# Attention scores computed three head pairs ahead of the top-k search instead of two, with six score buffers instead of five

## The chip, the cores and the metric

The kernel runs on one core of one Trainium2 chip. The metric is the device time of one execution in microseconds (us). Three executions of the kernel before took 788.19, 790.3 and 794.51 us, a median of 790.3 us. A smaller number is better.

## The reference

Three layers follow each other, on 1152 tokens (2 batches of 576) with 512 features (8 heads of 64):

```python
scores = scale * q @ k.T                        # per batch and head, 576 x 576
kth    = np.partition(scores, -32)[..., -32]    # the 32nd largest of each row
attn   = softmax(where(scores >= kth, scores, -1e9))
x      = attn @ v                               # back to 1152 x 512
h      = x @ w_in                               # 512 x 2048
x      = (h * tanh(softplus(h))) @ w_out        # 2048 x 512
x      = ((x @ w_a) * (x @ w_b)) @ w_out2       # 512 x 1536, twice, then back
```

The inputs are 8 bytes wide for the weights and 4 bytes wide for q, k and v.

## The kernel before

**Attention.** The 1152 rows of q are cut into nine tiles of 128 rows (tile 4 holds the last 64 rows of both batches), and the eight heads into four pairs. One (tile, pair) is a step; there are 36. A step has three parts:

- `scores` (lines 159 to 179). `prep_q` transposes q on TensorE (`pq`, L144), splits it into a high part on ScalarE (`qh`, L154) and a low part on VectorE (`ql`, L155). For tiles 0 and 4, `prep_k` also loads, splits and transposes that pair of k (L107 to L128; its low part is made by GpSimd for batch 0 and by VectorE for batch 1, and `ks`, `kr`, `km`, `kn` have one buffer each). Eight matmuls (sixteen for tile 4) into `psc` follow (L176), and four ScalarE copies bring them to the tile `s2` of the step (L178).
- `largest` (lines 181 to 199), the search. On VectorE four rounds of MAX8 (L192) for the two heads and three of match-and-replace (L195) find the 32 largest of each row: 8 and 6 passes over 576 columns.
- `weighted_sum` (lines 205 to 251). The masked exponentials are made on VectorE (L212) and ScalarE (L217 to L220), transposed on TensorE (`pe`, L227), copied (`et`, L228) and multiplied with v (`px`, L234). After a tile's fourth pair the row sums are applied (`x`, L250).

**Weights.** All 68 weight blocks arrive as 8-byte numbers and are turned into 4-byte ones by ScalarE, VectorE and GpSimd (`convert`, L283 to L306), stored in device memory, and loaded again each time they are used (`raw`, L325). Where a layer works in two parts, `weight` splits a block into `whl` on ScalarE or VectorE (L332, L334) and GpSimd (L335).

**The two feed-forward layers.** `gated` and `bilinear` run three times (`PLAN`): over tiles 0, 1, 2 (the first layer as tiles 0 and 1, then tile 2), over 3, 4, 5, and over 6, 7, 8. The matmuls are L362 (into `ph`) and L369 (into `acc` and `po`). A group's gate needs `x` of its tiles, its bilinear layer the transposed results (`pt`, L351).

**What sets the order.** The program writes the three streams of work down interleaved: `together` draws a quarter of a step from `attention` and a block of weights or of a layer in turn, by the quotas of `STEPS`. `attention` (lines 253 to 268) writes the scores of the first `ABUF[7]` steps before the first search. Then each step writes its search in four rounds; after round 0 it writes the weighted sum of the step before, and after round 1 the scores of the step `ABUF[7]` later. A planner in the build then gives each engine its fixed order: what is written earlier goes first, and `PRI` moves parts forward in that order (scores by 200 places, L160; weighted sums by 300, L202; layer activations by 30; the end of a tile by 100), as far as operands and buffers allow. On the chip each engine works through its order strictly and waits for its operands. All DMAs are issued from SP. `ps` (L78) gives three PSUM banks to `pq`, `pk`, `pr`, `psc`, `pe`, `px`, `prs` and `pt` together. `ABUF[0]` is the number of `s2` buffers (L169), `ABUF[1]` that of `wk`, `ABUF[2]` that of `e2`, `ABUF[4]` that of `qh` and `ql`.

```python
ahead = [scores(*z) for z in steps[:ABUF[7]]]
...
    if r == 0 and tail:
        weighted_sum(*tail)
    if r == 1 and i + ABUF[7] < len(steps):
        ahead.append(scores(*steps[i + ABUF[7]]))
```

Of the kernel before, what the change touches and what calls it, by code (L numbers as in the profile page):

```python
# [33 lines left out]

SIGN = (4, 4)

ABUF = (5, 3, 2, 1, 2, 3, 1, 2)
COPIES = (0, 0, 0, 1, 4, 2)

CONV = (26, 28, 20, 2)  # L40
# [11 lines left out]
def topk_attention_mlps(ctx: ExitStack, tc: tile.TileContext, q, k, v, w, out):  # L52
# [22 lines left out]
    wp = ctx.enter_context(tc.tile_pool(name="wp", bufs=1))  # L75
    ep = ctx.enter_context(tc.tile_pool(name="ep", bufs=ABUF[5]))
    dp = ctx.enter_context(tc.tile_pool(name="dp", bufs=1, space=DRAM))
# [28 lines left out]
    def prep_k(b, hp):  # L106
        ks = wp.tile([P, 2, J, D], F32, name="ks", bufs=BUFS[4])  # L107
        kr = wp.tile([R, 2, D], F32, name="kr", bufs=BUFS[4])
        for s in range(2):
            nc.sync.dma_start(ks[:, s], k[b, 2 * hp + s, 0:SM, :].rearrange("(p j) d -> p j d", j=J))  # L110
        nc.sync.dma_start(kr, k[b, 2 * hp:2 * hp + 2, SM:S, :].rearrange("h p d -> p h d"))
        km = wp.tile([P, 2, J, 2, D], F32R, name="km", bufs=BUFS[4])
        kn = wp.tile([R, 2, 2, D], F32R, name="kn", bufs=BUFS[4])
        for z, raw in ((km, ks), (kn, kr)):
            high, low = (z[..., i, :] for i in range(2))
            nc.scalar.copy(high, raw)
            (nc.gpsimd, nc.vector)[KSUB[b]].tensor_sub(low, raw, high.bitcast(F32))
        for s in range(2):
            kk = kks[:, (b * H + 2 * hp + s) % (H + 2), :]
            pk = bank("pk")  # L120
            for j in range(J):
                nc.tensor.transpose(pk[:, j * P:(j + 1) * P], km[:, s, j].rearrange("p z d -> p (z d)").bitcast(F32),
                                    ident)
            pr = bank("pr", R)
            nc.tensor.transpose(pr, kn[:, s].rearrange("p z d -> p (z d)").bitcast(F32), ident[:R, :R])
            for src, o, n in ((pk, s * R, SM), (pr, SM * (1 - s), R)):
                nc.scalar.copy(kk[:, o:o + n], src)  # L127
            KK[b, 2 * hp + s] = kk  # L128
# [12 lines left out]
    def prep_q(t, hp):  # L141
# [4 lines left out]
        for b, o, n in ([(t // (J + 1), 0, P)] if t != J else [(b, b * R, R) for b in range(B)]):  # L146
            qh = att.tile([P, 2, P], F32R, name="qh", bufs=ABUF[4])
            ql = att.tile([P, 2, P], F32R, name="ql", bufs=ABUF[4])
            if n != P:
# [13 lines left out]
    def scores_(t, hp):  # L163
# [3 lines left out]
        if t in (0, J):  # L167
            prep_k(t // J, hp)
        s2 = att.tile([P, 2, S], F32, name="s2", bufs=ABUF[0])  # L169
        for s in range(2):  # L170
# [10 lines left out]
    def largest(s2):  # L181

        e2 = att.tile([P, 2, S], F32, name="e2", bufs=ABUF[2])
        wk = att.tile([P, 2, S], F32, name="wk", bufs=ABUF[1])
        m8 = att.tile([P, 2, TOPK], F32, name="m8")
# [332 lines left out]
```

## Time and profile before

| | |
|---|---|
| runs | 788.19, 790.3, 794.51 us; median 790.3 |
| profiled execution | 790.78 us, of which the span of the instructions is 789.0 |
| busy over the span | TensorE 690.1 us (87%), VectorE 571.1 (72%), ScalarE 550.8 (70%), GpSimd 466.0 (59%) |
| granted TensorE clock, mean | 0.935 |

Busy shares are means over stages that differ, so the rows below cut the span into stages. A matmul's duration is modelled and overlaps the next one's, so that the sum of durations is more than the time they take. A number in brackets after an instruction is the time its engine stood idle before it, with what ended that.

### The profile page before, as it was taken

The page shows a single profiled execution, that of the slowest core. Times are in us where ns is not written, and L with a number is a line of the kernel's source. Part 1 is how long each engine was busy: PE and PEld are TensorE (multiplying, and loading weights), DVE is VectorE, ACT ScalarE, POOL GpSimd, SP SyncE. Part 2 cuts the span into 40 slices and gives each one's busy share as a digit, 9 for nine tenths or more (in the row PEclk, how much of TensorE's full clock was granted, in tenths as well). Part 3 has the DMA queues.
Part 4 walks back from the last instruction along what each step waited for, and adds up shares of the span by engine and source line. Part 5 has one row for each costly group of instructions (what it writes and reads, how often), then busy time and mean ns, then how long its engine had stood idle before and what let it go on. Part 6 is the DMA issues. An engine that isn't in the chain of part 4 may idle for free. (4 is left out here: it accounts for less than half of the span.)

```text
span 789.0 us, 12393 instructions
## 1 busy us (share of the span) xinstructions
PE 690.1 (87%) x3988; PEld 572.0 (72%) x3988; DVE 571.1 (72%) x1152; ACT 550.8 (70%) x1262; POOL 466.0 (59%) x390
## 2 busy tenths in 40 slices
PE   3565657789977988999999999988999999989997
PEld 2444535556664757889897888867979999969996
DVE  3999999976798789986679998998601276523331
ACT  5889888888997996666668998976524275553232
POOL 6756566676775751456554465552648767665661
PEclk9987667799997998999999999997999999999999
DMA  8987665889989973134334234221403454433411
GB/s 244 288 272 251 209 204 182 225 256 304 354 282 325 342 232 111 54 95 133 94 90 129 78 90 112 80 68 55 134 15 108 119 173 125 131 105 107 125 51 40
DMA packets 79537, 126.12 MB, mean 160 GB/s; under 512 B 27504, under 2 KB 31600, under 8 KB 79472
## 3 DMA queue, kind: packets, MB, share of 16 engines
q1 hardware_dynamic: 79472, 125.33, 52.3%
q8 instruction: 31, 0.51, 0.3%
q14 instruction: 34, 0.28, 0.1%
HBM read 105.12 MB, written 20.19 MB: 159 GB/s over the span
## 5 line engine op out<-in xcount | busy, mean ns | idle before, releaser
L335 POOL TENSOR_TENSOR whl<-raw,whl 128x512 fp32r<-128x512 f32 x164 | 215.3, 1321 | 161.5 <-ACT whl L334 126.6
L192 DVE MAX8 m<-wk 128x8 f32<-128x576 f32 x216 | 158.5, 749 | 1.1
L362 PE MATMUL ph<-yh,whl 128*128 128x384 f32 x576 | 154.6, 340 | 0.7 <-ACT yh L344 0.7
L298 POOL TENSOR_TENSOR w<-w,w 128x512 int32<-128x512 int32 x68 | 89.0, 1309 | 77.8 <-DVE w L295 40.5
L362 PEld LDWEIGHTS ph<-yh,whl 128*128 128x128 f32 x576 | 105.6, 190 | 4.0 <-ACT yh L344 1.6
L195 DVE MATCH_REPLACE8 wk<-m,wk 128x576 f32<-128x576 f32 x144 | 106.4, 741 | 0.0
L362 PE MATMUL ph<-yl,whl 128*128 128x384 f32 x288 | 98.4, 342 | 0.1
L299 POOL TENSOR_TENSOR w<-w,w 128x512 f32<-128x512 f32 x68 | 89.7, 1322 | 7.0 <-ACT w L297 2.2
L234 PE MATMUL px<-et,v 128*64 128x128 f32 (+1 forms) x800 | 76.6, 297 | 17.3 <-ACT et L228 17.0
L334 ACT CAST whl<-raw 128x512 fp32r<-128x512 f32 x113 | 69.3, 622 | 28.8 <-PE ph L362 16.2
L234 PEld LDWEIGHTS px<-et,v 128*64 128x64 f32 x800 | 53.1, 151 | 40.1 <-ACT et L228 26.8
L377 POOL TENSOR_TENSOR gl<-m,gh 128x384 fp32r<-128x384 f32 x52 | 55.5, 1067 | 42.9 <-ACT gh L376 12.1
L362 PE MATMUL ph<-xh,whl 128*128 128x384 f32 x256 | 71.6, 340 | 0.7 <-DVE m L409 0.7
L192 DVE MAX8 m<-s 128x8 f32<-128x576 f32 x72 | 53.9, 751 | 25.2 <-ACT s L178 24.7
L176 PE MATMUL psc<-kks,qh 128*128 128x288 f32 x160 | 57.2, 377 | 13.8 <-ACT kks L127 7.9
L434 DVE TENSOR_TENSOR m<-ph,e 128x384 f32<-128x384 f32 x36 | 19.9, 554 | 67.9 <-PE ph L362 54.9
L376 ACT CAST gh<-m 128x384 fp32r<-128x384 f32 x68 | 34.8, 511 | 48.8 <-DVE m L434 27.6
L227 PE MATMUL pe<-ident,e 128*128 128x128 f32 x324 | 55.7, 305 | 14.7 <-ACT e L220 7.4
L176 PE MATMUL psc<-kks,ql 128*128 128x288 f32 x160 | 51.4, 352 | 11.5 <-DVE ql L155 11.2
L178 ACT COPY s<-psc 128x288 f32<-128x288 f32 x144 | 52.0, 402 | 13.2 <-PE psc L176 12.4
L293 ACT ACTIVATE w<-w 128x512 f32<-128x512 f32 x68 | 46.5, 684 | 20.3 <-DMA w<-in_w_dram 13.5
L228 ACT COPY et<-pe 128x384 f32<-128x384 f32 x108 | 50.3, 487 | 14.6 <-PE pe L227 14.5
(90 smaller groups left out, 1520.3 us busy)
## 6 DMA issues: line engine op xcount, KB each, us to landing
raw<-ws SPq DMA_DIRECT2D x229, 256.0 KB, 2.8
w<-in_w_dram SPq DMA_DIRECT2D x68, 512.0 KB, 4.8
ws<-w SPq DMA_DIRECT2D x68, 256.0 KB, 4.5
qr<-in_q_dram SPq DMA_DIRECT2D x16, 256.0 KB, 4.2
ks<-in_k_dram SPq DMA_DIRECT2D x16, 128.0 KB, 4.3
v<-in_v_dram SPq DMA_DIRECT2D x16, 128.0 KB, 3.9
out_dram<-o SPq DMA_DIRECT2D x8, 256.0 KB, 3.0
qr<-in_q_dram SPq DMA_DIRECT2D x4, 128.0 KB, 8.1
```

Of the source, the lines that this page charges most:

```text
L176: nc.tensor.matmul(psc, qq[:, s, :], kk[:, a * HS:(a + 1) * HS], start=(n == 0), stop=(n == len(parts) - 1))
L178: nc.scalar.copy(s2[:, s, a * HS:(a + 1) * HS], psc)
L192: nc.vector.max(m8[:, s, got], src[:, s, :])
L195: nc.vector.match_replace(wk[:, s, :], m8[:, s, got], src[:, s, :], NEG)
L227: nc.tensor.transpose(pe[:, i, :], ef[:, n * P:(n + 1) * P], ident)
L234: nc.tensor.matmul(px[s * D:(s + 1) * D, o:o + n], vt[b][:, 2 * hp + s, j, :] if j < J else v4[b][:, hp, s, :], et[:, i if j < J else J, o ...
L298: nc.gpsimd.tensor_tensor(wi, wi, count, op=ALU.add)
L299: nc.gpsimd.tensor_mul(wf, wf, highf)
L334: nc.scalar.copy(wh, raw)
L335: sub().tensor_sub(wl, raw, wh.bitcast(F32))
L362: nc.tensor.matmul(ph, a, x, start=(i == 0), stop=(i == len(mm) - 1))
L377: sub().tensor_sub(gl, g, gh.bitcast(F32))
```

## The change

Two numbers of `ABUF`: `s2` gets six buffers instead of five, and scores are written three steps ahead of the search instead of two. The scores of step 2 move ahead of the first search, and those of every later step move ahead by the search and the weighted sum of one step, with all that was written between.

```diff
-ABUF = (5, 3, 2, 1, 2, 3, 1, 2)
+ABUF = (6, 3, 2, 1, 2, 3, 1, 3)
```

## Rows read from the trace of the kernel before

**Rows 1.** Busy times by stage: PE, PEld, DVE, ACT, POOL, then granted clock, DMA share, GB/s
```profile
16.00:136.00 120.00, 72.85 (x392) 53.48 (x390) 117.10 (x249) 101.84 (x245) 77.42 (x62) 0.77 0.77 239
136.00:294.00 158.00, 135.90 (x692) 95.03 (x691) 129.19 (x259) 143.24 (x312) 107.43 (x90) 0.91 0.89 288
294.00:315.00 21.00, 18.32 (x158) 15.57 (x157) 19.29 (x44) 14.97 (x43) 5.00 (x11) 0.84 0.42 121
315.00:540.00 225.00, 216.42 (x1451) 187.92 (x1450) 200.19 (x415) 173.93 (x429) 121.44 (x100) 0.98 0.33 91
540.00:600.00 60.00, 59.97 (x367) 51.46 (x366) 27.23 (x55) 28.94 (x66) 30.89 (x26) 0.97 0.25 75
600.00:789.00 189.00, 180.39 (x919) 164.15 (x917) 74.25 (x129) 78.19 (x153) 115.33 (x90) 0.99 0.38 109
```

**Rows 2.** VectorE's waits (total, times, longest): 0 to 165, 165 to 320, 320 to 570
```profile
DVE m L192 <- ACT s L178: 2.5, 3, 1.7
...
DVE m L192 <- ACT s L178: 7.0, 6, 1.6
...
DVE m L192 <- ACT s L178: 15.2, 9, 4.9
```

**Rows 3.** Timeline of ScalarE and VectorE, a search's start and the last two steps
```profile
362.58 0.76 DVE L192 MAX8 m<-s 128x8 f32<-128x576 f32 x1 [4.86 <-ACT s L178]
...
548.22 0.78 ACT L218 ACTIVATE e<-s,nk 128x576 f32<-128x576 f32 x1
...
553.87 1.01 ACT L178 COPY s<-psc 128x288 f32<-128x288 f32 x3 [0.96 <-PE psc L176]
...
558.80 0.40 ACT L178 COPY s<-psc 128x288 f32<-128x288 f32 x1
...
559.24 0.76 DVE L192 MAX8 m<-s 128x8 f32<-128x576 f32 x1
```

**Rows 4.** The page's group of MAX8: busy, mean ns of one, idle before
```profile
L192 DVE MAX8 m<-wk 128x8 f32<-128x576 f32 x216 | 158.5, 749 | 1.1
```

**Rows 5.** Attention's matmuls from 315 to 540 us, by line
```profile
L234 PE MATMUL px<-et,v 128*64 128x128 f32 (+1 forms) x360 | 27.1, 263 | 1.4 <-ACT et L228 1.4
...
L227 PE MATMUL pe<-ident,e 128*128 128x128 f32 x133 | 19.9, 272 | 0.2 <-ACT s L178 0.2
...
L176 PE MATMUL psc<-kks,qh 128*128 128x288 f32 x60 | 18.1, 318 | 0.5 <-ACT qh L154 0.5
L176 PE MATMUL psc<-kks,ql 128*128 128x288 f32 x60 | 16.6, 316 | 3.9 <-DVE ql L155 3.8
...
L144 PE MATMUL pq<-ident,qr 128*128 128x128 f32 x30 | 6.6, 300 | 0.0
```

**Rows 6.** A piece of the chain that ended last: start, length
```profile
719.13 3.32 PE ph L362 x19
```

**Rows 7.** Timeline, tile 8's result and the first matmul that reads it
```profile
591.59 0.69 DVE L250 TENSOR_TENSOR x<-xr,prs 128x512 f32<-128x512 f32 x1 [8.57 <-ACT xr L238]
...
630.69 0.34 PE L362 MATMUL ph<-xh,whl 128*128 128x384 f32 x1
```

**Rows 8.** Timeline, tile 1's result and the start of the first gate
```profile
134.43 0.68 DVE L250 TENSOR_TENSOR x<-xr,prs 128x512 f32<-128x512 f32 x1
...
135.49 0.53 PE L176 MATMUL psc<-kks,ql 128*128 128x288 f32 x2 [2.35 <-DVE ql L155]
...
136.33 0.92 PE L362 MATMUL ph<-xf,w 128*128 128x256 f32 x3
```

**Rows 9.** The stretch from 520 to 540 us, columns as in Rows 1
```profile
520.00:540.00 20.00, 15.33 (x96) 11.69 (x95) 19.72 (x39) 15.51 (x39) 8.15 (x7) 0.83 0.19 54
```

**Rows 10.** Timeline of VectorE and TensorE in that stretch
```profile
533.38 0.41 DVE L155 SCALAR_TENSOR_TENSOR ql<-pq,qh 128x256 fp32r<-128x256 f32 x1
...
533.85 0.85 PE L176 MATMUL psc<-kks,ql 128*128 128x288 f32 x2 [2.77 <-DVE ql L155]
```

## The prediction

> **What bounds the kernel now.** I read the busy times by stage first, because the shares over the whole span hide that the bound changes [rows 1]. From 16 to 136 us VectorE is busy for 117.1 of 120 us: the searches of tiles 0 and 1, with the weight conversions among them, set the pace. From 136 to 294 no engine is full (ScalarE 143.2 and TensorE 135.9 of 158), but the DMA share is 0.89: the weights' conversion and reloading bind. From 294 to 315 nearly everything is attention, at a granted clock of 0.84. From 315 on TensorE is the bound, with 216.4 of 225 us, 60.0 of 60 and 180.4 of 189.
>
> Is a busy TensorE a full one? A piece of the final chain has 19 matmuls of 384 columns in 3.32 us [rows 6], 0.175 us each with no gap. So it is full there, and after 315 us only a gap that closes, or TensorE work that leaves this stage, can save time.
>
> Then I looked for what the change acts on: how long the search waits for scores, and how far ahead scores really are. VectorE waits 2.5 us for them up to 165, 7.0 from there to 320 and 15.2 from 320 to 570 [rows 2], 24.7 in all. And the scores are not two steps ahead when they run: the last step's copies begin at 553.87, after the step before it last read its own scores at 548.22, and the search starts its second head at 559.24, with the copy at 558.80 [rows 3]. The lead of the written order is used up by the planned order. So the lead is short in fact, and the buffers are not: at the end two of the five would do.
>
> **The change, part by part.**
>
> *The sixth buffer* costs and brings nothing by itself: a scores tile is free before the next but one is filled [rows 3]. The Trainium skill's page Perfetto Trace Analysis, section Optimization Strategy, says that gaps which repeat on an engine can mean that there is no room for the next tile. By that rule the buffer would be worth the waits, up to 24.7 us; the trace disagrees with it here, since the tile was free 5.65 us before it was filled (553.87 − 548.22).
>
> *Three steps written before the first search.* Step 2's k loads, splits, transposes, two matmul groups and four copies now stand ahead of the first search in the order. Moved on SP are its two `ks` loads and `kr`, past the early weight loads; on GpSimd its two subtractions, past conversions. `ks` has one buffer, so they come behind step 1's, and the first search needs step 0 alone: 0 us. Bounds: 2.5 us gained, if all waits up to 165 go [rows 2], or the same amount lost, if ScalarE serves step 2 where step 0's search waits.
>
> *The first stage* is VectorE's, and its work is unchanged but for one `ql` more, 0.41 us [rows 10], that is now done before tile 1 ends. This end matters: `x` of tile 1 comes at 134.43 and the first gate matmul at 136.33, with a score step in front of it for which TensorE waited 2.35 us [rows 8]. With the change that place is held by the next step's scores. I take 0; bounds from −2.4 us (the wait is gone) to +2.8 (0.41 + 2.35: one more of the kind).
>
> *From 136 to 315* the scores stand one step further ahead of the layer's matmuls, so the search can run a step further before 315. Room for that is there: a search is 14 passes of 0.749 us [rows 4], the replacing ones taken at the same length, so 10.5 us, and VectorE idles for 158 − 129.2 = 28.8 us of it [rows 1], 7.0 of it for scores. TensorE idles 22.1 us there, enough for the step's matmuls. The DMA-bound layer in between does not become shorter.
>
> *From 315 on* attention is then one step further, and TensorE has one step less to do. The attention lines add up to 27.1 + 19.9 + 18.1 + 16.6 + 6.6 = 88.3 us [rows 5] for 15 steps (120 score matmuls, 8 each): 5.9 us per step by durations. These overlap: a matmul of 0.34 us advances the queue by 0.175 [rows 6, 7], so about half, 2.9 us, is TensorE time. I take 2.9 us gained; the ends are 0 (no step moves) and 5.9.
>
> *The 15.2 us of waits after 320* I cost at nothing. TensorE covers them: while VectorE waits, it works on the layers. If the search ends earlier, nothing starts earlier: the last tile's `x` is made at 591.59 and first multiplied at 630.69 [rows 7]. What is late next is the layers' own matmuls.
>
> *The queue moves.* Each step's query load (two DMAs on SP where a tile begins), `ql` on VectorE, memsets on GpSimd (tile 4) and four copies on ScalarE go past one search and one weighted sum, and past some weight reloads and splits. The number of each is unchanged. ScalarE pays 1.4 us per step for the copies (1.01 + 0.40) [rows 3], which it paid before. It idles 51 us in the stage after 315, so 0; without that cover a copied step could delay a gate by those 1.4 us.
>
> **Sum**, against the profiled execution's 790.8 us (789.0 of span; the median of the runs is 790.3): 790.8 − 2.9 = 787.9 us.
>
> **The rivals.**
>
> *Nothing moves* (0.24). The planner ate a lead of two steps, and could eat three: then the scores still end when the search wants them. For it: the copies that end as the search starts [rows 3]. Against: where TensorE is the bound it chooses between scores and layer matmuls by written place, and that place changes. Time 790.8, give or take 4.
>
> *The wait goes from VectorE to TensorE* (0.18), the slower side. TensorE keeps its order, so `psc` blocks all behind it until VectorE has made `ql`. That is seen from 520 to 540 us [rows 9, 10]: VectorE is busy for 19.7 of 20 us, `ql` is done only from 533.38, and TensorE stands still for 2.77 us; in these 20 us it idles 4.7 us, and the clock of 0.83 takes 20 × 0.17 = 3.4 more, 8.1 together. Take away VectorE's 15.2 us of waits and it is this dense more often, since now a search follows a search. It decides when VectorE has no idle time left ahead of a `ql` while TensorE has no layer work in its order ahead of `psc`. One such place more gives 798.9, two give 807. Against it: in 315 to 540 the matmuls waited only 3.8 us in all for `ql` [rows 5], and a `ql` that is asked for a step earlier has more time. I put it at 801.
>
> *The waits do come back* (0.20). If scores pace the whole attention and attention paces the layers, 7.0 + 15.2 = 22.2 us go, and 768.6 us is left; half of that, 779.7, is what I would expect of this case, since the layers bound part of it. For it: the waits lie where the search has nothing else, and the transitions of 294 to 315 and 520 to 540 have TensorE gaps that attention work could fill. Against: the pitch of 0.175 us [rows 6]. The Trainium skill (Perfetto Trace Analysis, Identifying the Most-Contended Engine) warns that matmul busy time tells little of a TensorE at its limit and wants the share of weight loads instead. By that rule 187.9 of 225 us, 84%, leaves room, and the late waits alone would give 790.8 − 15.2 = 775.6; the trace at 0.175 us for 384 columns back to back speaks against it.
>
> **How the numbers follow.** My forecast has 0.38, with a range of its own of 783 to 791. A measurement of this kernel tells a change from none at about 1%, 782.4 to 798.2. Faster: the whole of the last rival and 0.04 of the forecast's tail, 0.24. Slower: 0.18. Within 1%: 0.58. The range goes down to 778, which leaves out about half of the last rival, and up to 800, which leaves out about half of the slower one, together some 0.18.
>
> **What would show it.** Right: VectorE's waits for scores after 165 us well under 22 us; the copies a search or more ahead of it; the search's last pass well before 567; fewer attention matmuls after 315; TensorE as full as now. Nothing moves: copies still end as the search begins. The slower rival: more idle before `psc` for `ql`, and stretches with a clock under 1 after 315. The forecast is wrong if the first gate matmul moves from 136.3 by more than 3 us either way, which I cost at nothing, or if the gaps at 294 to 315 and 520 to 540 change by more than that.

## The result and the profile after

The changed kernel takes 799.0 us in the median of four runs (798.4 to 799.4) against 790.42 for the kernel before: a ratio of 1.0102, 95% interval [1.006, 1.0144]. It is slower by 1%, where 787.9 was predicted. Its profiled execution took 798.4 us, with a span of 796.6, 7.6 us more than before. The busy times of the engines are nearly those of before (TensorE 689.5 us, VectorE 572.1, ScalarE 552.0): no work was added, so the loss is waiting, or work at a lower clock.

Where it is, the stages tell. These are the windows of the changed kernel, cut as in [rows 1] with the same columns (PE, PEld, DVE, ACT, POOL, granted clock, DMA share, GB/s):

```profile
16.00:136.00 120.00, 73.60 (x400) 55.71 (x401) 118.82 (x253) 101.80 (x246) 71.59 (x57) 0.84 0.74 227
136.00:294.00 158.00, 132.70 (x683) 91.29 (x681) 135.40 (x270) 141.41 (x309) 109.18 (x95) 0.92 0.88 290
294.00:315.00 21.00, 13.54 (x83) 9.18 (x83) 10.84 (x20) 12.26 (x32) 8.34 (x10) 0.75 0.52 168
315.00:540.00 225.00, 218.26 (x1498) 190.87 (x1498) 204.02 (x428) 174.93 (x432) 117.26 (x97) 0.98 0.31 88
```

The third line stands out. From 294 to 315 us TensorE does 83 matmuls instead of 158, at a clock of 0.75 instead of 0.84, and VectorE works 10.8 us instead of 19.3. Up to 136 the engines do nearly the work of before (the clock is 0.84 there instead of 0.77), and the stage after 315 is as full as before.

A good mark for the end of this stretch is the moment at which VectorE splits the transposed result of tile 2 (`yl`, L346), with which the first bilinear layer starts; I call it the first start. In the timeline of VectorE it stands at 331.00 in the changed kernel and stood at 317.63 before:

```profile
331.00 0.69 DVE L346 TENSOR_TENSOR yl<-pt,yh 128x512 fp32r<-128x512 f32 x1
```
```profile
317.63 0.67 DVE L346 TENSOR_TENSOR yl<-pt,yh 128x512 fp32r<-128x512 f32 x1
```

From 270 us to it, first in the changed kernel and then in the kernel before:

```profile
270.00:331.00 61.00, 43.64 (x279) 31.24 (x277) 44.95 (x91) 43.61 (x112) 25.93 (x27) 0.83 0.54 176
```
```profile
270.00:317.63 47.63, 41.46 (x301) 32.42 (x300) 42.03 (x90) 38.75 (x101) 18.63 (x25) 0.93 0.59 191
```

TensorE idles 61.0 − 43.64 = 17.4 us against 6.2, and the clock takes 61 × 0.17 = 10.4 against 47.6 × 0.07 = 3.3. (The two overlap where TensorE idles at a low clock, so they do not add up to the loss.) The same line gives the rest: in the second and third layer, where it is the split of the first of three tiles, it stands at 549.12 and 712.30 (before 538.25 and 704.31). So the way to the first start costs 13.4 us more, first to second 2.5 less (218.1 for 220.6), second to third 2.9 less (163.2 for 166.1), and the rest 0.4 less: 7.6 us in all.

The place itself, from the timeline of the changed kernel:

```profile
290.68 0.65 ACT L405 ACTIVATE e<-e 128x512 f32<-128x512 f32 x1
290.75 0.27 PE L125 MATMUL pr<-ident,kn 64*128 64x64 f32 x1
...
292.23 0.63 ACT L334 CAST whl<-raw 128x512 fp32r<-128x512 f32 x1
...
293.52 0.67 ACT L406 ACTIVATE e<-e 128x512 f32<-128x512 f32 x1
...
296.52 1.55 DVE L117 TENSOR_TENSOR km<-ks,km 128x512 fp32r<-128x512 f32 x1 [3.16 <-ACT km L116]
...
297.17 0.74 ACT L407 ACTIVATE e<-e,half 128x512 f32<-128x512 f32 x1
...
298.00 1.35 DVE L117 TENSOR_TENSOR kn<-kr,kn 64x128 fp32r<-64x128 f32 x1
298.32 0.63 ACT L408 ACTIVATE m<-e 128x512 f32<-128x512 f32 x1
299.28 0.67 DVE L409 SCALAR_TENSOR_TENSOR m<-m,ph 128x512 f32<-128x512 f32 x1
300.00 6.02 PE L369 MATMUL acc<-raw,m 128*128 128x512 f32 x8 [8.98 <-DVE m L409]
305.46 0.70 PE L176 MATMUL psc<-kks,qh 128*128 128x288 f32 x1
...
307.55 0.76 DVE L192 MAX8 m<-s 128x8 f32<-128x576 f32 x1 [7.60 <-ACT s L178]
```

TensorE stands still for 8.98 us before the last matmuls of tile 2's first layer (L369). These need the last gate group's result, made by four activations on ScalarE (L405 to L408) and one operation of VectorE (L409). From the first activation's start to the last one's end they take 8.3 us (290.68 to 298.95), because splits of weights (L334), conversions and the preparation of tile 4's keys stand between them; L409 stands behind two key differences (L117). The scores of step 18 (the third of tile 4; steps are counted from 0) stand behind the same matmuls, though the last of its keys was copied at 297.1, and the search waits 7.60 us for them. Before, the four activations came close together:

```profile
285.08 0.63 ACT L405 ACTIVATE e<-e 128x512 f32<-128x512 f32 x1 [0.50 <-DVE e L404]
285.74 0.63 ACT L406 ACTIVATE e<-e 128x512 f32<-128x512 f32 x1
286.41 0.72 ACT L407 ACTIVATE e<-e,half 128x512 f32<-128x512 f32 x1
288.35 0.61 ACT L408 ACTIVATE m<-e 128x512 f32<-128x512 f32 x1
289.74 3.70 PE L369 MATMUL acc<-raw,m 128*128 128x512 f32 x8 [0.90 <-DVE m L409]
```

That is 3.9 us, and the matmuls behind them waited 0.90, since TensorE had step 17's scores to do meanwhile. The pause also costs clock: after it the same eight matmuls take 6.02 us instead of 3.70 (the granted clock is 0.61 from 300 to 306 in the changed kernel, and was 1.00 from 291 to 300 before).

The waits that the change could be hoped to remove did not go. VectorE's waits for scores in the changed kernel, from 0 to 165, 165 to 320 and 320 to 580 us (total, times, longest):

```profile
DVE m L192 <- ACT s L178: 2.1, 1, 2.1
...
DVE m L192 <- ACT s L178: 10.4, 5, 7.6
...
DVE m L192 <- ACT s L178: 18.1, 6, 4.0
```

30.6 us in all, against 24.7 [rows 2].

What moved is one score step and nothing else. Counted up to the first start, TensorE has 200 score matmuls behind it (L176) instead of 192, but the same 162 transposes (L227) and 366 products (L234) of the weighted sums. From the first to the second start it is 120 score matmuls in both, and after that none instead of eight.

### The profile page after: what moved, and what is told of

It is laid out like the page before. It is cut to its first block, busy times and chain, and to the rows that moved or that the text cites. A ratio compares the mean times of both kernels' runs of the same rounds, so it can differ in the third digit from the quotient of the medians.

```text
span 796.6 us, 12392 instructions
## 1 busy us (share of the span) xinstructions
PE 689.5 (87%) x3988; PEld 570.2 (72%) x3988; DVE 572.1 (72%) x1152; ACT 552.0 (69%) x1262; POOL 465.8 (58%) x390
## 5 line engine op out<-in xcount | busy, mean ns | idle before, releaser
L334 ACT CAST whl<-raw 128x512 fp32r<-128x512 f32 x113 | 69.9, 621 | 41.3 <-PE ph L362 25.8
L299 POOL TENSOR_TENSOR w<-w,w 128x512 f32<-128x512 f32 x68 | 91.5, 1346 | 7.9 <-ACT w L297 2.7
L234 PE MATMUL px<-et,v 128*64 128x128 f32 (+1 forms) x800 | 75.4, 296 | 18.2 <-ACT et L228 16.3
L234 PEld LDWEIGHTS px<-et,v 128*64 128x64 f32 x800 | 52.7, 150 | 40.8 <-ACT et L228 26.5
L192 DVE MAX8 m<-s 128x8 f32<-128x576 f32 x72 | 53.3, 749 | 30.6 <-ACT s L178 30.5
L176 PE MATMUL psc<-kks,qh 128*128 128x288 f32 x160 | 53.3, 358 | 12.8 <-ACT qh L154 7.1
L227 PE MATMUL pe<-ident,e 128*128 128x128 f32 x324 | 54.0, 304 | 7.8 <-ACT s L178 7.7
L178 ACT COPY s<-psc 128x288 f32<-128x288 f32 x144 | 51.8, 401 | 11.6 <-PE psc L176 10.8
L369 PE MATMUL po<-whl,gh 128*128 128x512 f32 x216 | 59.6, 398 | 0.2 <-ACT gh L376 0.2
L176 PE MATMUL psc<-kks,ql 128*128 128x288 f32 x160 | 48.7, 338 | 12.2 <-DVE ql L155 12.2
```

What stands on the lines that cost most here:

```text
L176: nc.tensor.matmul(psc, qq[:, s, :], kk[:, a * HS:(a + 1) * HS], start=(n == 0), stop=(n == len(parts) - 1))
L192: nc.vector.max(m8[:, s, got], src[:, s, :])
L227: nc.tensor.transpose(pe[:, i, :], ef[:, n * P:(n + 1) * P], ident)
L234: nc.tensor.matmul(px[s * D:(s + 1) * D, o:o + n], vt[b][:, 2 * hp + s, j, :] if j < J else v4[b][:, hp, s, :], et[:, i if j < J else J, o ...
L299: nc.gpsimd.tensor_mul(wf, wf, highf)
L334: nc.scalar.copy(wh, raw)
```

## The experiments

All but three of them use one frame: the number of steps ahead becomes a function of the step `m`, with six score buffers. With 3 for every `m` it is the changed kernel, with 2, but for the sixth buffer, the kernel before.

```diff
-ahead = [scores(*z) for z in steps[:ABUF[7]]]
+todo, lead = list(enumerate(steps)), lambda m: ...
+ahead = [scores(*todo.pop(0)[1]) for m in range(len(steps)) if m < lead(m)]
...
-    if r == 1 and i + ABUF[7] < len(steps):
-        ahead.append(scores(*steps[i + ABUF[7]]))
+    while r == 1 and todo and todo[0][0] - lead(todo[0][0]) <= i:
+        ahead.append(scores(*todo.pop(0)[1]))
```

Steps 16 to 19 are tile 4, which also prepares the keys of batch 1. Step 20 is the one that the change moves ahead of the first start, step 35 the one ahead of the second. The table gives each kernel's median, its ratio to the kernel before on the same chip, and from one profiled execution the first, second and third start and the span:

| kernel | lead | us | ratio, 95% | first | second | third | span |
|---|---|---|---|---|---|---|---|
| before | 2 | 790.4 | | 317.6 | 538.3 | 704.3 | 789.0 |
| after | 3 | 799.0 | 1.0102 [1.006, 1.0144] | 331.0 | 549.1 | 712.3 | 796.6 |
| e1 | 3, tile 4: 2 | 796.7 | 1.0105 [1.0057, 1.0153] | 316.8 | 544.7 | 710.0 | 793.2 |
| e2 | 2, tile 4: 3 | 797.5 | 1.0092 [1.0058, 1.0125] | 317.6 | 545.2 | 709.4 | 795.3 |
| e3 | 3 for 0 to 15 | 790.7 | 0.9998 [0.9981, 1.0015] | 313.3 | 539.2 | 705.7 | 790.3 |
| e4 | 3 from 20 on | 802.0 | 1.0154 [1.0116, 1.0193] | 324.5 | 552.1 | 715.9 | 801.5 |
| e5 | 3 for 20 alone | 797.7 | 1.0088 [1.0062, 1.0115] | 323.0 | 545.6 | 710.8 | 795.3 |
| e6 | 3 from 21 on | 801.9 | 1.0152 [1.0123, 1.018] | 318.9 | 551.8 | 715.4 | 798.6 |
| e7 | 3 for 0 to 19 | 802.8 | 1.0154 [1.0127, 1.018] | 326.4 | 551.0 | 717.2 | 801.5 |
| e8 | 3, step 20: 2 | 807.3 | 1.0211 [1.0187, 1.0234] | 326.2 | 558.3 | 721.3 | 806.9 |
| e9 | 2, steps 19, 34: 1 | 791.5 | 0.9999 [0.9983, 1.0015] | 309.2 | 538.9 | 701.5 | 786.3 |
| e10 | 3 for 0 to 15; 19, 34: 1 | 786.0 | 0.9937 [0.9916, 0.9958] | 307.8 | 537.9 | 700.8 | 784.0 |
| e11 | 3 for 0 to 15 and 21 to 34 | 792.1 | 1.002 [1.0003, 1.0037] | 312.1 | 540.0 | 704.6 | 790.3 |
| e12 | 3, five buffers | 799.3 | 1.0107 [1.0084, 1.0131] | 332.8 | 550.9 | 714.1 | 798.5 |
| e13 | after, six splits moved | 810.0 | 1.0264 [1.0236, 1.0292] | 331.1 | 559.3 | 722.9 | 807.1 |
| e14 | 3 from 16 on | 803.9 | 1.0182 [1.0152, 1.0211] | 321.6 | 549.6 | 713.4 | 799.7 |
| e15 | 2, step 19: 1 | 798.0 | 1.0121 [1.0088, 1.0155] | 311.5 | 546.7 | 711.0 | 794.2 |
| e16 | after, both queues shorter | 806.3 | 1.0194 [1.0153, 1.0235] | 324.7 | 554.9 | 721.0 | 804.2 |
| e17 | 3 for 0 to 15; 34: 1 | 790.6 | 0.9997 [0.9976, 1.0019] | 315.2 | 538.9 | 705.1 | 790.7 |

The three starts come from one execution each, and executions scatter. It can be seen where two kernels have the same order of instructions: the changed kernel and e12 have one order on TensorE, VectorE, ScalarE and GpSimd from first to last, and the first start at 331.0 and 332.8; e3, e11 and e17 have one order up to it, and it stands at 313.3, 312.1 and 315.2; so have e9 and e15, with 309.2 and 311.5. A mark is good to some 2 us. Where two kernels share their order up to some instruction, the difference is better counted from there.

The theories: A, the loss is one place at the end of tile 2's gate; B, conversions come late because early scores ran ahead; C, the lead costs throughout the last stage; D, a score step moved in front of a layer's start costs its whole chain of waits there and gives back only its matmul time later; E, the planned order merely scatters.

**Which steps cost.**

```diff
-lambda m: 3
+lambda m: 2 if 16 <= m < 20 else 3
```


> Scores three steps ahead everywhere except for tile 4 (steps 16 to 19), which stay two ahead. Theory A (the loss is made in one place, at the end of tile 2's gate near 286 to 331 us, where tile 4's scores and their k preparation, now a step earlier, stand among the last activation group on ScalarE and behind its matmuls on TensorE): the 9.0 us gap ahead of the last gate matmuls of tile 2 falls under 3 us, and the time is 788 to 793 us. Theory B (the loss is made before 280 us: scores that run ahead in the first stage take time from the weight conversions, which end 12 us later, and the late conversions hold the last group): the gap stays over 6 us, 796 to 801 us. Theory C (scores a step ahead cost TensorE waits in the last stage, after 332 us): 795 to 800 us with the first gap gone.

```diff
-lambda m: 2
+lambda m: 3 if 16 <= m < 20 else 2
```


> Scores two steps ahead everywhere except for tile 4 (steps 16 to 19), which run three ahead. Theory A: the gap ahead of tile 2's last gate matmuls is 6 to 10 us as in the changed kernel, 796 to 802 us. Theory B: conversions end where they did before (near 280 us), no gap over 2 us, 788 to 792 us. Theory C: 788 to 792 us.

```diff
-lambda m: 3
+lambda m: 3 if m < 16 else 2
```


> Scores three steps ahead for steps 0 to 15 (tiles 0 to 3), two ahead from tile 4 on. Theory A: 787 to 793 us, no gap over 3 us ahead of tile 2's last gate matmuls. Theory B: the late conversions are made by these steps, 796 to 801 us. Theory C: 788 to 792 us.

```diff
-lambda m: 2
+lambda m: 2 if m < 20 else 3
```


> Scores two steps ahead up to tile 4, three ahead from tile 5 (step 20) on, so that only the last stage differs from the kernel before. Theories A and B: 788 to 792 us, the start of the first bilinear layer unmoved (317 to 318 us for its last transposed part). Theory C: 795 to 800 us, TensorE idle after 332 us up by 5 us or more.

The lead for steps 0 to 15 alone costs nothing (e3) and even brings the first start forward by 4.4 us. Tile 4 alone does not delay the first start (e2, 317.6) and still ends 1% slower. Without tile 4 the 13 us up to the first start are gone (e1, 316.8) and the total is hardly better. So theory A names the right place for the first start, but tile 4 alone does not make its gap, as A expected of e2, and the total does not hang on that place: behind the first start e1 takes 476.4 us, the changed kernel 465.6. e4 fits none of the three: its first start moved, and 802.0 is above C's 795 to 800.

**Splitting the late steps.**

```diff
-lambda m: 2
+lambda m: 3 if m == 20 else 2
```


> Scores two steps ahead as in the kernel before, but step 20 (the first of tile 5) alone three ahead: its scores then stand in front of the first bilinear layer instead of among it. Theory D (a score step that is moved in front of a layer's start, where TensorE has no layer matmuls to do, costs its whole chain of transposes, ScalarE copy, VectorE split and matmuls there, and gives back only its matmul time later): the last transposed part of tile 2 comes at 323 to 326 us as with steps 20 to 35 ahead, 317.6 before, and the time is 793 to 799 us. Theory E (the loss is scatter of the planned order that has no place of its own): any of 788 to 800 us, the first layer's start not tied to it.

```diff
-lambda m: 2
+lambda m: 3 if m > 20 else 2
```


> Scores two steps ahead up to step 20, three ahead from step 21 on, so that nothing is planned otherwise before the first bilinear layer. Theory D: its start stays at 317 to 319 us; step 35 now stands in front of the second bilinear layer, so some 2 to 6 us are lost there: 792 to 797 us. If the loss is all in front of the first bilinear layer: 788 to 792 us. Theory C (the lead costs TensorE waits throughout the last stage): 797 to 803 us, as with step 20 ahead too.

```diff
-lambda m: 3
+lambda m: 3 if m < 20 else 2
```


> Scores three steps ahead for steps 0 to 19, two ahead from step 20 on. If tile 4 ahead together with the earlier steps makes the 9.0 us gap of the changed kernel: a gap of 6 to 10 us in front of tile 2's last gate matmuls again, 795 to 800 us. If the later steps make the loss (theory C or D with step 20): no such gap beyond 3 us, 788 to 793 us.

```diff
-lambda m: 3
+lambda m: 2 if m == 20 else 3
```


> The changed kernel, but step 20 alone two ahead. Theory D: one score step less in front of the first bilinear layer, so its last transposed part comes 4 to 8 us earlier than 331.0 and the time is 791 to 796 us. If the gap ahead of tile 2's last gate matmuls (theory A) is all of it: gap and time unchanged, 797 to 800 us.

Step 20 in front of the first start delays it by 5.4 us (e5 against before), 5.6 (e4 against e6), 3.6 (e1 against e3) and 4.8 (after against e8). Counted from the last matmul before the orders of a pair part on TensorE, it is 6.6, 6.6, 4.4 and 5.8. The timeline of TensorE in e5 shows where they go:

```profile
313.34 0.41 PE L144 MATMUL pq<-ident,qr 128*128 128x128 f32 x2 [0.24 <-DMA qr<-in_q_dram]
314.30 0.53 PE L176 MATMUL psc<-kks,qh 128*128 128x288 f32 x2 [0.56 <-ACT qh L154]
316.86 0.53 PE L176 MATMUL psc<-kks,ql 128*128 128x288 f32 x2 [2.03 <-DVE ql L155]
...
318.07 1.06 PE L351 MATMUL pt<-ident,y 128*128 128x128 f32 x4
```

In the kernel before, the transposes of the result (L351) follow on step 19's scores at once:

```profile
314.03 0.30 PE L176 MATMUL psc<-kks,ql 128*128 128x288 f32 x1
314.17 0.60 PE L351 MATMUL pt<-ident,y 128*128 128x128 f32 x4
```

The scores are ten matmuls, but they take 5.0 us (313.10 to 318.07): the transposed q, its high part and its low part come one after the other from three engines, TensorE waits 0.24 + 0.56 + 2.03 = 2.8 us in between, and the last matmuls run at the lower clock (0.71 granted on the mean from 316.86 to 318.07), 0.24 us apart instead of 0.13. That is D at the first start. Of the four totals of this group D has e5's alone: e6, e7 and e8 took 802 to 807 us, and e8, with a score step less in front of the start, was to take 791 to 796. Its converse, that the time comes back as matmul time, is weak in the runs: second to third start took 164.0 us on average in the nine kernels with step 35 ahead, 164.9 in the ten with it behind, and the groups spread over 3 and 4 us.

e7 has the wait of 8.97 us in front of tile 2's last matmuls and e8 one of 8.99; of the first eight kernels no other has it. Given steps 0 to 15, adding tile 4 costs 326.41 − 313.25 = 13.2 us at the first start; without them it cost 0 (e2). The order shows why. In e3 that gate group is as late (its four activations take 8.6 us, 287.55 to 296.16), but TensorE still has step 18's scores to do meanwhile:

```profile
292.15 0.58 PE L176 MATMUL psc<-kks,qh 128*128 128x288 f32 x1 [2.43 <-ACT whl L334]
...
294.73 0.58 PE L176 MATMUL psc<-kks,ql 128*128 128x288 f32 x1 [0.47 <-DVE ql L155]
...
298.01 4.08 PE L369 MATMUL acc<-raw,m 128*128 128x512 f32 x8
```

In the changed kernel step 17's scores are long done and step 18's stand behind those matmuls.

**Fewer steps in front of the starts, and the buffer.**

```diff
-lambda m: 2
+lambda m: 1 if m in (19, 34) else 2
```


> Lead two as before, but one for steps 19 and 34, so that one score step fewer stands in front of each layer's first bilinear matmul: the opposite of the change at the two starts. D (a score step in front of a layer's start costs its latency there, about 5 us, and gives back only some 1.9 us of matmul time where TensorE is full): first bilinear start 317.6 - 5 = 312.6, second 5 to 12 us less in its stage, + 1.9 for each step done later; 790.6 - 6 to - 13, so 777 to 785. Rival S (the search then starves: two steps are asked for one search of 10.5 us later): first start unchanged at 316 to 319, longer waits of VectorE for scores, 792 to 801. Rival E (only scatter of the planned order): between 784 and 798 with the stage up to the first start within 1 us of 317.6.

```diff
-lambda m: 2
+lambda m: 3 if m < 16 else 1 if m in (19, 34) else 2
```


> Lead three for steps 0 to 15, one for 19 and 34, two for the rest. D: first start at 313.25 - 5 = 308, no gap of 9 us behind the last gate group of tile 2, second start as in the run before, 776 to 786. S: tile 4's last step is late for the search, the gain up to the first start stays at 4 us and is lost later, 790 to 800. E: 784 to 798.

```diff
-lambda m: 3
+lambda m: 3 if m < 16 or 20 < m < 35 else 2
```


> Lead three for steps 0 to 15 and 21 to 34, two for 16 to 20 and 35: three steps ahead everywhere but at tile 4 and in front of the two layer starts. D: nothing of the loss is left, first start at 313 as with 0 to 15 alone, 790 give or take 3. C (the lead costs all through the stage after 315): 796 to 802, as with lead three from step 21 on (801.9). E: up to 6 us either way, with the stages that have the same work apart by that.

```diff
-ABUF = (6, 3, 2, 1, 2, 3, 1, 3)
+ABUF = (5, 3, 2, 1, 2, 3, 1, 3)
```


> Lead three for all steps, but five score buffers as before. If the sixth buffer does nothing by itself: 799, ratio to the kernel before 1.008 to 1.014, the same stages as the changed kernel within 0.5 us. If the sixth buffer lets scores through earlier: slower than 799 by 3 us or more, with copies that wait for a buffer of VectorE's.

e9 has the first start 8.4 us earlier (6.1 counted from the last matmul that it has in common with the kernel before), as D wanted, but reaches the second at 538.9 like the kernel before, and its ratio is 0.9999: D's total of 777 to 785 fails. The second layer's gate waits for `x` of tile 5, and this comes at 419.65 in e9, 421.65 before. That is no gain, since e9 was 2.3 us ahead already at that matmul: TensorE had done less attention by its first start and did it then. e10 is the one kernel that beats both, by 0.6%, at the edge of D's range of 776 to 786. e11 is at 1.002, outside C's 796 to 802: three steps ahead cost nothing there, with tile 4 and the steps ahead of the two starts left at two. But e6, with the lead from step 21 to 35 and none before, took 801.9, as C had it, and in pairs that part at 323 to 336 us this lead delays the second start by 4.6 (e4 against e5), 7.4 (e8 against e7) and 12.2 us (e6 against before). Whether e11 is spared by the lead of steps 0 to 15 or by leaving out step 35 was not run; e8 and e7, which both have the early lead, speak for step 35. e12 is the changed kernel over again, in the same order throughout: the sixth buffer does nothing at lead three.

**The place itself.**

```diff
-        if made[1] % 4 < COPIES[phase[0]]:
+        if made[1] % 4 < COPIES[phase[0]] or (1, 0, 0) <= key < (1, 2, 2) and phase[0] == 1:
```


> The changed kernel, but the first six high copies of weights for the bilinear layer (0.52 us each on ScalarE) are made by VectorE, which waits there anyway. The order of TensorE up to the first bilinear start is that of the changed kernel. If ScalarE's work in front of the last gate group sets the gap of 9.0 us before its matmuls: the four activations of that group take 8.3 - 6 x 0.52 = 5.2 us, the gap is about 6 us, first start 331 - 3 = 328. Rival (VectorE's km and kn differences, which stand in front of the gate's last operation, or a load sets it): the gap stays at 8.5 to 9.5 and the start at 330 to 332. What comes after is in another order, so the total is no test: 793 to 800.

ScalarE's part came out as worked out: 290.34 to 295.64, 5.3 us. But the wait grew to 9.99 us, on the rival's side and beyond its 9.5, and the total of 810.0 lies above the 793 to 800 given. The timeline of e13 shows VectorE's queue in ScalarE's place:

```profile
294.04 2.71 DVE L332 CAST whl<-raw 128x512 fp32r<-128x512 f32 x2
296.67 1.74 DVE L117 TENSOR_TENSOR km<-ks,km 128x512 fp32r<-128x512 f32 x1
298.34 1.34 DVE L117 TENSOR_TENSOR kn<-kr,kn 64x128 fp32r<-64x128 f32 x1
...
299.94 0.67 DVE L409 SCALAR_TENSOR_TENSOR m<-m,ph 128x512 f32<-128x512 f32 x1
300.67 5.78 PE L369 MATMUL acc<-raw,m 128*128 128x512 f32 x8 [9.99 <-DVE m L409]
```

In the changed kernel both queues had ended within 0.4 us of each other (298.95 and 299.28), so shortening one could not help. And VectorE's grew by more than ScalarE's lost: the six copies took 0.41 to 1.51 us each on it, 6.0 together, beside GpSimd's work, where they had been worked out at 0.52 each on ScalarE.

```diff
-        if made[1] % 4 < COPIES[phase[0]]:
+        if made[1] % 4 < COPIES[phase[0]] or phase[0] == 1 and key < (1, 1, 0):
...
-            (nc.gpsimd, nc.vector)[KSUB[b]].tensor_sub(low, raw, high.bitcast(F32))
+            (nc.gpsimd, nc.vector)[KSUB[b] if hp != 3 else 0].tensor_sub(low, raw, high.bitcast(F32))
```


> The changed kernel, with the high copies of the first three weights of the bilinear layer on VectorE and step 19's key differences on GpSimd: both queues are shorter in front of the last gate group of tile 2, and TensorE's order up to the first bilinear start is the changed kernel's. If the two queues together set the gap: ScalarE's four activations take 8.3 - 4 x 0.52 = 6.2 us, VectorE's last gate operation follows at once, the gap is 6.5 to 7 us and the first start 328 to 329. If neither does: 8.5 us or more, 330 or later. The order after that is another, so the total is no test (793 to 812).

With both queues shorter the wait shrinks to 7.48 us, and the matmuls start 3.7 us earlier. Of these, 2.2 us are scatter, since TensorE ends its last work before the pause that much earlier, in the same order:

```profile
295.57 0.69 DVE L409 SCALAR_TENSOR_TENSOR m<-m,ph 128x512 f32<-128x512 f32 x1 [2.04 <-ACT m L408]
296.31 5.14 PE L369 MATMUL acc<-raw,m 128*128 128x512 f32 x8 [7.48 <-DVE m L409]
```

The first start comes 6.3 us earlier (324.7), some 4 without the scatter, where 2 to 3 were expected, and the wait is half a microsecond longer than expected: ScalarE's four activations still take 7.0 us instead of the 6.2 worked out, 0.7 of it a wait for a weight to be loaded, and VectorE waits for them (2.04). So the gate group's two queues set a part of this wait at least: 1.5 us went when both were shorter, and none in e13, which shortened one and lengthened the other. Only this run shows it, and none took away the rest.

**What the lead of the early steps has to do with it, and where e10 gains.**

```diff
-lambda m: 2
+lambda m: 2 if m < 16 else 3
```


> Lead three for steps 16 to 35, two for 0 to 15. If the gap of 9 us needs the early lead: no wait above 2.5 us in front of a gate group of tile 2, first start at 317.6 + 5 for step 20, 322 to 325, total 797 to 803 as with lead three from step 20 on. If tile 4's lead alone makes it: first start 330 or later.

```diff
-lambda m: 2
+lambda m: 1 if m == 19 else 2
```


> Lead two as before, one for step 19 alone. First start at 309.2 as with 19 and 34 late. If the time of the next gate's x (419.65 there, 421.65 before) is what holds: x of tile 5 again at 419 to 421, and the second start at 538 to 541, so the 8.4 us are gone at the second gate; total 788 to 793. If the late step 34 was what gave it back: second start at 530 to 534 and a total of 781 to 786.

```diff
-lambda m: 2
+lambda m: 3 if m < 16 else 1 if m == 34 else 2
```


> Lead three for steps 0 to 15, one for step 34, two for the rest. If the gain of the run with 19 and 34 late (785.97) was made at the first start: first start 313.25, total 788 to 793. If at the second: first start 313.25, the second at 534 to 539 and the total 784 to 788.

e14 completes the square: tile 4 and step 20 ahead, without steps 0 to 15, give 321.6 (5.8 us for step 20 against e2, from the last common matmul), no such wait and 803.9 us, both just outside the 322 to 325 and 797 to 803 expected. The gap needs both. A sign of what the early lead does there is the last conversion on ScalarE (L293): at 276.5 in the kernel before and 289.4 in the changed one, so that conversions stand in the late gate group's way; it ran late in the early-lead kernels e1, e3, e7 and e8 as well (284.9 to 290.4), which is B's half of the matter; but e3 loses nothing by it.

e15 and e17 were to split e10's gain. e15 has the early first start (311.5) and `x` of tile 5 on time (422.35), but then a second start at 546.7, which neither expectation had, and is 1.2% slower than before. Set beside e9 this is D at the second start. Up to there TensorE has the same order in both, and e15 runs 2.7 us behind. Then e15 has step 34's scores to do, which e9 has put off, and it waits for `ql` as e5 did at the first start; here e15, then e9:

```profile
541.28 0.85 PE L176 MATMUL psc<-kks,ql 128*128 128x288 f32 x2 [2.14 <-DVE ql L155]
...
542.89 1.06 PE L351 MATMUL pt<-ident,y 128*128 128x128 f32 x4
```
```profile
534.99 0.66 PE L351 MATMUL pt<-ident,y 128*128 128x128 f32 x4
```

The second start comes 7.8 us later, 5.2 of them since the orders parted. The same step put off in e17, against e3, brings 1.4. e17 has the second start of e9 and e10 and the total of the kernel before, which excludes a gain by step 34 on top of steps 0 to 15 alone; its first start is 315.2, 2 us behind e3's in the same order. So e10's 0.6% needs both the early lead, which e9 lacks, and the late step 19, which e17 lacks; whether it needs the late step 34 was not run. In the profiled executions it lies, against e17, behind the second start (246.1 us from there to the end for 251.8); what makes it is open.

## Why the prediction was wrong

**Where it failed.** The step that failed is "so the search can run a step further before 315", with the price of nothing for the stage from 136 to 315 behind it. Room there was, though of the 7.0 us of waits that it counted into 136 to 294, which are those of 165 to 320, only 5.5 lie there. And the second search of tile 4 (step 17) did start earlier, at 277.26 in the changed kernel for 290.76:

```profile
277.26 0.74 DVE L192 MAX8 m<-s 128x8 f32<-128x576 f32 x1
```
```profile
290.76 0.76 DVE L192 MAX8 m<-s 128x8 f32<-128x576 f32 x1 [1.07 <-ACT s L178]
...
305.20 0.76 DVE L192 MAX8 m<-s 128x8 f32<-128x576 f32 x1 [1.52 <-ACT s L178]
```

But the next one (step 18) starts no earlier for that, at 307.55 for 305.20, since its scores stand behind the late gate group. Only the scores of one step came in front of the first start, no search and no weighted sum. The way to the first start, of which the prediction said only that the layer in it becomes no shorter, became 13.4 us longer. By kernels that differ in one thing, this is −4.4 for steps 0 to 15 (e3), +13.2 for tile 4 on top of them (e7) and +4.6 for step 20 and those behind it (after against e7): 13.4, each good to some 2 us.

This accounts for the first start, where the changed kernel loses. It does not account for its whole time: e1 has next to nothing of this delay and still takes 796.7 us.

**The queue moves.** The prediction asked what a copy on ScalarE would cost without cover, put it at 1.4 us a step, and looked for that cover after 315 only. It was gone before 315, at the end of tile 2's gate, and there not 1.4 us but a whole gate group was late: four activations in 8.3 us instead of 3.9, and 9.0 us of an empty TensorE. ScalarE idles 16.6 us from 136 to 294, but not there.

**The term of −2.9 us.** It was made for a whole step of attention; a score step alone moved. After the first start the changed kernel needs 465.6 us against 471.4, a gain of 5.8. Cut into pieces of about 5 us (length less busy time, and length times the missing clock), about 4.3 us of it are less idle time and a higher clock, and about 1.5 us is less TensorE work. This is an estimate: by the same reckoning kernels with the same steps left differ by up to 4 us, and the eight with step 20 ahead lie 1.5 us below the eight without on the mean. It is about what the step's ten matmuls cost where TensorE is full, with the eight score matmuls 0.13 us apart. And the 4.3 are no constant of the lead: e12, in the same order, has them too, but the other seventeen kernels take 471 to 483 us for this part, with a score step more or less in it.

**What held.** The sixth buffer: nothing, by e12. The repeated gaps of VectorE were no want of room. The rule of the Trainium skill that the prediction cited (Perfetto Trace Analysis, Optimization Strategy) speaks of the engine that should be saturated. VectorE was that up to 136 us, and of its 24.7 us of waits only 2.5 lay up to 165, so no run here goes against it. Three steps before the first search and the first stage's end: the waits up to 165 went from 2.5 to 2.1 us, and the first gate matmul came at 134.39 for 136.33 [rows 8], inside the 3 us allowed:

```profile
132.05 0.53 PE L176 MATMUL psc<-kks,qh 128*128 128x288 f32 x2 [0.47 <-ACT qh L154]
...
132.43 0.67 DVE L250 TENSOR_TENSOR x<-xr,prs 128x512 f32<-128x512 f32 x1
...
134.39 5.21 PE L362 MATMUL ph<-xf,w 128*128 128x256 f32 x16 [1.81 <-ACT xf L344]
```

That VectorE's late waits are covered held too: they grew to 18.1 us, and tile 8's `x` (598.39) still lies 40 us ahead of its first matmul (638.85), as in [rows 7].

**The rivals.** "The wait goes from VectorE to TensorE" had the side and nearly the time (801), and the right sort of mechanism, TensorE held at its place in the order. Its place was wrong, so that its time came near is luck, and so is it that the range, drawn up to 800 for this rival, holds the 799.0: the wait is for a gate group behind ScalarE and VectorE, not for `ql` from 520 to 540. That stretch got better, and its gap moved behind it:

```profile
520.00:540.00 20.00, 19.39 (x135) 16.11 (x134) 19.96 (x42) 18.58 (x46) 12.55 (x11) 1.00 0.30 80
540.00:560.00 20.00, 16.43 (x97) 13.47 (x97) 17.03 (x36) 13.55 (x33) 6.04 (x5) 0.91 0.36 119
```

Against 15.33 us busy at 0.83 [rows 9] this is the later second start, not a gain. "Nothing moves" and "the waits come back" both fell: the order moved, and the waits rose from 24.7 to 30.6 us. The text's own sign was right: it called the forecast wrong if the gap at 294 to 315 changed by more than 3 us, and TensorE's idle time there went from 2.7 to 7.5 us (at 520 to 540 from 4.7 to 0.6, where the gap only moved).

**What stays open.** Why the changed kernel, slower by 8.6 us, is slower by just that. Its delay at the first start is followed by the shortest rest of all, and e1 and e2, without the delay, lose 5.0 and 6.2 us behind it against the kernel before. From first to second start the same score steps, 21 to 35, take 218.1 us in the changed kernel, the same again in e12, and 230.1 in e16, so this belongs to the order and is no scatter of executions. In all kernels TensorE stays nearly full (at most 3.8 us idle) until tile 5's `x`. From that `x` to the second start it takes 113.3 us in e12, 113.4 in the changed kernel, 116.6 in the kernel before and up to 125.2 in e5, and idle time and low clock there go from 6.3 us to 18.9 (e6). Which instruction of the order decides was not tried; for this part of the loss theory E stands.

## What to carry to other kernels

Written lead is not lead: ask which instructions end up in front of which. Here one score step came in front of a layer's start, where it costs its chain over three engines (4 to 7 us at the first start), and left a full TensorE, where it is worth about 1.5. Look at the transitions first, where an in-order engine has nothing else to do; the cover of a moved step must be there at the spot, not on the average of a stage. And where a planner makes the order anew, a small edit scatters the total by 1% after the spot one understands, so test single steps before believing a cause, and compare two kernels from the instruction at which their orders part.

## What the runs showed of the hardware

VectorE's subtraction of the keys (L117, two inputs of 128 x 512) took 0.69 us in e14 and 1.55 in the changed kernel, its small companion 0.28 and 1.35:

```profile
297.62 0.69 DVE L117 TENSOR_TENSOR km<-ks,km 128x512 fp32r<-128x512 f32 x1 [1.08 <-ACT km L116]
298.24 0.28 DVE L117 TENSOR_TENSOR kn<-kr,kn 64x128 fp32r<-64x128 f32 x1
```

In the changed kernel GpSimd ran six subtractions back to back at that time; in e14 it had just ended three:

```profile
293.81 7.89 POOL L335 TENSOR_TENSOR whl<-raw,whl 128x512 fp32r<-128x512 f32 x6
```

The Trainium skill's page SBUF — State Buffer (section SBUF: two separate sides) says that VectorE with two inputs from SBUF and GpSimd share a pair of ports that one of them holds for a whole instruction. The trace agrees: the two subtractions lasted 1.9 us longer together, while one of GpSimd takes 7.89 / 6 = 1.3 us. In the traces of all nineteen kernels the two took at most 0.69 and 0.28 us wherever no arithmetic of GpSimd ran at the same time, and every longer one ran beside it. The weight copies on VectorE (L332) behave alike: 0.41 to 0.43 us without, up to 1.51 beside GpSimd, as in e13. That is part of the late gate group, and no term of the prediction had it.
